# Block 1 of an attention and PReLU kernel: tile steps spaced out, loads between norm products, q of batch 0 first

## The chip, the cores and the metric

The kernel runs on one core of a Trainium2 chip. The metric is device time in microseconds of one execution; 301.3 us is the median of the five runs of the kernel before.

## The reference

Inputs q, k, v have shape (8, 8, 576, 64): batch, heads, sequence, head dimension. The result has 4608 rows of 512.

```python
kv = einsum('bhsd,bhse->bhde', k, v)
out = einsum('bhsd,bhde->bhse', q, kv)
rms = sqrt(mean(out * out, axis=-1, keepdims=True) + 1e-06)
x = (out / rms * g_norm).transpose(0, 2, 1, 3).reshape(4608, 512)
h = x @ w_in                                   # 512 -> 2048
g = maximum(h, 0) + alpha * minimum(h, 0)
result = g @ w_out                             # 2048 -> 512
```

## The kernel before

Each engine's instructions are in an order written out by hand. PE is TensorE, DVE VectorE, ACT ScalarE, POOL GpSimd; SP issues the transposes and stores, POOL the loads.

**Blocks.** The 4608 rows of x are cut into nine blocks w = 0 to 8 of 512 rows. A batch has 576 rows, so a block holds parts of two batches. A block's first layer is 16 groups g (`m1_group`): four matmuls of 128x512 into a PSUM buffer h_ps (three of them, in turn), then ACT writes m_sb = relu(-h) (L474), and DVE writes gt = m_sb * beta + h (L476). The second layer of the block before (`y_mm`, L494) is put between the groups of the block, four matmuls after each group. Block 1 is different: the second layer of block 0 was mostly done ahead of it, so between its 16 groups there is little else for PE.

**Attention.** For batches 0 and 1 (`NB_PE = 2`) it is done at the start, with transposed outputs: `step_t` transposes q on PE, `step_kv` makes k^T v of head pairs (L240) and masks it on DVE into kv_sb (L244), `step_ot` multiplies by q, `ssq_mm` and `norm` normalize. For the later batches it is done a block ahead, in tiles of 128 rows, in steps laid between the groups (`phase_steps`):

- `tile_a`: four matmuls into otm_ps on PE (L387), and the square on ACT.
- `tile_b`: the sums of squares by a DVE reduce (L399).
- `tile_c`: Ln and Exp on ACT, then rg = rstd * g on POOL (L411, the norm product).
- `tile_d`: xrow = otm_ps * rg on DVE (L420), and a DMA transpose of xrow on SP's queue into xm, the input of the next block (L425).

In one step, tile_b and tile_d come ahead of the group's own instructions, tile_c and step_kv behind its matmuls, tile_a at the end. Before the change, a tile's a, b with c, and d are in three steps in a row. Block 1 has the tiles of batch 2 that block 2 needs: three, with tile_a after groups 7, 8 and 9. kv of batch 2 is made behind group 5.

**Loads.** q, k, v are loaded with a cast to 16 bits by POOL's queue, two issues for each tensor of a batch (`load`: 64 partitions of five rows, 64 partitions of four). There are two stage buffers, so batch b + 2 takes the place of batch b. `regroup` copies q and k so that a pair of heads lies together (on DVE up to batch 2, on POOL after it, L106); `transpose_q` then transposes q by DMA into qtm. In block 1, POOL waits at `gate` (L677) for the transposed q of batch 2, then issues q and k of batch 3; its v follows behind group 9. Batch 4 is loaded in block 2 by six issues in a row ahead of group 6.

**Start.** Batch 0 is loaded in halves of four heads, in the order q, k, v, q, k, v. `keep_warm` issues matmuls whose result nobody uses. `spread_g` makes g_all, which tile_c reads, by one matmul (g_ps, L522) behind group 12 of block 0.

Of the kernel before, what the change touches and what calls it, by code (L numbers as in the profile page):

```python
# [9 lines left out]
FP32 = mybir.dt.float32  # L10
# [7 lines left out]
def kernel(  # L18
# [11 lines left out]
    nc = tc.nc  # L30

    B, H, S, D = q.shape
# [3 lines left out]
    P = 128  # L36
# [4 lines left out]
    TPP = S // P  # L41
    REM = S - TPP * P
    NT = TPP + 1
# [46 lines left out]
    def zero_rest(st):  # L90
        nc.vector.memset(st[REM:P, :, TPP, :], 0.0)

    def load(b, nm, h0=0, h1=H):
        st = stages[b % NBUF][nm][:, h0:h1]
        src = srcs[nm][b, h0:h1]
        nc.gpsimd.dma_start(
            out=st[0:REM].rearrange("p h t d -> p h (t d)"),
            in_=src[:, 0:LONG, :].rearrange("h (p t) d -> p h (t d)", t=NT),
        )
        nc.gpsimd.dma_start(  # L100
            out=st[REM:P, :, 0:TPP, :].rearrange("p h t d -> p h (t d)"),
            in_=src[:, LONG:S, :].rearrange("h (p t) d -> p h (t d)", t=TPP),
        )

    def regroup(b, nm, h0=0, h1=H, eng=None):
        (eng or nc.vector).tensor_copy(  # L106
            out=bufs[b % NBUF][nm][:, :, h0:h1, :].rearrange("p t h d -> p h t d"),
            in_=stages[b % NBUF][nm][:, h0:h1],
        )
# [6 lines left out]
        for nm in ("q", "k"):  # L116
            regroup(b, nm, eng=nc.gpsimd)

    for nm in "qkv":
        zero_rest(stages[0][nm])  # L120
    HH = H // 2
    load(0, "q", 0, HH)

    ident = const_p.tile([P, P], FP32, name="ident")
    make_identity(nc, ident[:])
    for h0 in (0, HH):
        for nm in "qkv":
            if (h0, nm) != (0, "q"):
                load(0, nm, h0, h0 + HH)

    mask32 = const_p.tile([P, P], FP32, name="mask32")
    nc.vector.memset(mask32[:], 0.0)
# [11 lines left out]
    nc.vector.tensor_copy(out=ident16[:], in_=ident[:])  # L144
    for nm in "kvq":
        zero_rest(stages[1][nm])

    g2col = const_p.tile([P, 1], FP32, name="g2col")
    nc.sync.dma_start(out=g2col[0:64, :], in_=g_norm[:].unsqueeze(1))
# [47 lines left out]
    def keep_warm(n):  # L197
        for i in range(n):
            nc.tensor.matmul(  # L199
                out=warm_ps[:], lhsT=mask16[:], rhs=warm16[:], start=True, stop=True,  # L200
            )
# [10 lines left out]
    def step_t(b, j, pool=(ps_s, "s"), eng=None):  # L212
        qs = pair_cols(b, "q", j)
        qt_ps = pool[0].tile([P, NT * P], FP16, name="qt_ps", tag=pool[1])
        for t in range(NT):
            nc.tensor.matmul(
                out=qt_ps[:, t * P : (t + 1) * P],
                lhsT=qs(t),
                rhs=ident16[:],
                is_transpose=True,  # L220
                start=(t == 0),
                stop=(t == NT - 1),
            )
        qts[b, j] = attn_p.tile([P, S], FP16, name="qt_sb", tag=f"qt{j}")
        if eng is nc.scalar:
            nc.scalar.copy(out=qts[b, j][:], in_=qt_ps[:, 0:S])
        else:
            nc.vector.tensor_copy(out=qts[b, j][:], in_=qt_ps[:, 0:S])
# [26 lines left out]

    def square(sq, ot_ps, shape, eng):
        if eng is nc.vector:
            o_sb = attn_p.tile(shape, FP32, name="o_sb", tag="rg")
            nc.vector.tensor_copy(out=o_sb[:], in_=ot_ps[:])
            nc.vector.tensor_mul(out=sq[:], in0=ot_ps[:], in1=o_sb[:])  # L260
        else:
            nc.scalar.activation(out=sq[:], in_=ot_ps[:], func=AF.Square)
# [141 lines left out]
    def tile_c(b, t):  # L404
        n, _, ss = tiles[b, t]
        nc.scalar.activation(  # L406
            out=ss[0:n], in_=ss[0:n], func=AF.Ln, bias=eps_t[0:n], scale=inv_d,
        )
        nc.scalar.activation(out=ss[0:n], in_=ss[0:n], func=AF.Exp, bias=0.0, scale=-0.5)  # L409
        rg = attn_p.tile([P, H, D], FP32, name="rg")  # L410
        nc.gpsimd.tensor_tensor(  # L411
            out=rg[0:n], in0=ss[0:n].unsqueeze(2).to_broadcast([n, H, D]),
            in1=g_all[0:n].unsqueeze(1).to_broadcast([n, H, D]), op=ALU.mult,
        )
        tiles[b, t][2] = rg
# [14 lines left out]
    def phase_steps(w):  # L430


        if w >= NW:
            return []
        todo = [(b, t) for b in range(NB_PE, min(B, w + 1)) for t in range(NT)
                if (b, t) not in done and b * S + t * P < (w + 1) * W]
        done.update(todo)
        steps = []

        kv_at = {NB_PE: 5, NB_PE + 1: 3}.get(w, 0)  # L440
        if w == NB_PE:
            n = NPAIR // JT
            for i in range(n + 1):
                m = [lambda i=i: step_tail_ot(i)] if i < n else []
                m += [lambda i=i: step_tail_ssq(i - 1)] if i > 0 else []
                steps.append(([], [], m))
        n = {NB_PE: 7, NB_PE + 1: 2}.get(w, 0)
        steps += [([], [], []) for i in range(n - len(steps))]
        for i in range(len(todo) + 2):
            a, b, d = ([todo[i - k]] if 0 <= i - k < len(todo) else [] for k in range(3))  # L450
            begin = [lambda x=x: tile_b(*x) for x in b] + [lambda x=x: tile_d(*x) for x in d]
            mid = [lambda x=x: tile_c(*x) for x in b]
            end = [lambda x=x: tile_a(*x) for x in a]
            steps.append((begin, mid, end))
        if w < B:
            steps[kv_at][1].append(lambda: step_kv(w))
        return steps
# [60 lines left out]

    def spread_g():

        g_ps = ps_y.tile([P, D], FP32, name="g_ps", tag="y")
        nc.tensor.matmul(  # L522
            out=g_ps[:], lhsT=ones32[0:D], rhs=diag[0:D], start=True, stop=True,
        )
        nc.vector.tensor_copy(out=g_all[:], in_=g_ps[:])
# [7 lines left out]
    )  # L533
    step_t(0, 0, H_POOL[0])
    step_t(0, 1, H_POOL[1], nc.scalar)
    regroup(0, "k", 0, HH)
    keep_warm(8)
    step_kv(0, 0, 2)
# [1 line left out]
    step_ot(0, 0)  # L540
    step_ot(0, 1)
    keep_warm(1)
    regroup(0, "q", HH, H)
    ssq_mm(0, 0)
    step_t(0, 2, H_POOL[2])
    step_t(0, 3, H_POOL[0])
# [8 lines left out]
        out=beta_sb[:], in0=alpha_ps[:], scalar1=-1.0, scalar2=1.0, op0=ALU.mult, op1=ALU.add,  # L555
    )
    ssq_mm(0, 1)
    regroup(0, "k", HH, H)
    norm(0, 0)
    keep_warm(3)  # L560
    step_kv(0, 2, 4)
    keep_warm(2)
    load_batch(2)
# [22 lines left out]
              13: (ps_s, "s")}  # L586
    for g in range(5, NF):
        m1_group(0, g, others.get(g))
        if g == 12:
            spread_g()  # L590

# [42 lines left out]
    ssq_mm(1, 3, S_POOL)  # L634
    norm(1, 2)
    ahead(11, NF)
    norm(1, 3)
    regroup(2, "q")
    transpose_q(2)
    for a in range(TPW - 1):  # L640
        y_out(ys[a], 0, a, nc.vector if a == 1 else None)

# [5 lines left out]
    for w in range(1, NW):  # L648
        steps = phase_steps(w + 1)
        for g in range(NF):  # L650
            if g == LOAD_G and 3 < w + 2 < B:
                load_batch(w + 2)
            a, part = divmod(g, TPW)
            parts = range(part * TPW, (part + 1) * TPW)
            if w == 1:
                a, y = TPW - 1, ys[TPW - 1]
                parts = [LATER + g] if LATER + g < NF else []
            begin, mid, end = steps.pop(0) if steps else ([], [], [])
            for f in begin:
                f()  # L660
            m1_group(w, g)
            for f in mid:
                f()
            if 0 in parts:
                pool, tag = ((ps_y, "y"), (ps_s, "s"))[a % 2]
                y = pool.tile([P, W], FP32, name="y_ps", tag=tag)
            for gg in parts:
                y_mm(y, w - 1, a, gg)
            if NF - 1 in parts:
                y_out(y, w - 1, a)  # L670
            for f in end:
                f()
            if (w, g) == (1, 3):


                gate = const_p.tile([1, 1], FP16, name="gate")
                nc.gpsimd.tensor_copy(out=gate[:], in_=qtms[2][0:1, 0, 0:1])  # L677
                load(3, "q")
                load(3, "k")
                regroup(2, "k")  # L680
            if (w, g) == (1, 9):
                load(3, "v")
            if g == (13 if w == 1 else LOAD_G + 3) and w + 2 < B:
                regroup_batch(w + 2)
            if g == (15 if w == 1 else NF - 3) and w + 2 < B:
                transpose_q(w + 2)
# [43 lines left out]
```

## Time and profile before

| | us |
|---|---|
| Runs shown | 301.42, 300.75, 300.70, 301.44, 301.30 |
| Median | 301.3 |
| Profiled execution | 301.42 |
| Its span, first to last instruction | 299.3 |
| PE busy | 284.0 (95%) |
| DVE busy | 169.6 (57%) |
| ACT busy | 152.7 (51%) |
| POOL busy | 97.8 (33%) |

The span lies inside the profiled execution; the 2.1 us around it hold no instruction. Busy shares are averages over stages: the start is bound by loads, from block 2 on PE is full. A stage's own rows say what bounds it.

### The profile page before, as it was taken

To read this page: it belongs to the slowest core of one execution; us is meant where nothing else is said; L and a number is where in the kernel's file an instruction comes from. 1 tells how busy PE (TensorE), PEld (TensorE's weight loads), DVE (VectorE), ACT (ScalarE), POOL (GpSimd) and SP (SyncE) were. 2 spreads that over 40 slices of the span, in tenths; PEclk is the share of its full clock that TensorE was granted. 3 is DMA by queue.
4 is the path that set the end of the run, shared out by engine and by line. 5 is a ranking of instruction groups with operands and counts; after the bars stand their busy time and mean duration, and the time that the engine had idled before them with its cause. 6 is when DMAs were issued, how large, how long until landed. Compare 5 with 4: busy or idle time off the path is not lost.

```text
span 299.3 us, 4290 instructions
## 1 busy us (share of the span) xinstructions
PE 284.0 (95%) x1552; PEld 138.4 (46%) x1552; DVE 169.6 (57%) x262; ACT 152.7 (51%) x297; POOL 97.8 (33%) x109
## 2 busy tenths in 40 slices
PE   5889999987999999999999999999999999999994
PEld 2444454542453454445544544454445444444443
DVE  5468846785485458445954584468546744344200
ACT  1458355773475457435843573368347644443311
POOL 8843410349059415541466164515002300000000
PEclk9999999995999999999999999999999999999998
DMA  6999999999329943993399449926211411112232
GB/s 81 167 206 204 199 206 198 192 194 170 68 63 150 229 103 81 154 227 70 81 133 227 107 79 142 248 59 90 61 35 37 96 35 37 35 37 51 54 71 70
DMA packets 66228, 35.54 MB, mean 119 GB/s; under 512 B 32784, under 2 KB 61728, under 8 KB 66208
## 3 DMA queue, kind: packets, MB, share of 16 engines
q0 software_dynamic: 29664, 18.35, 44.5%
q1 hardware_dynamic: 36384, 16.80, 27.5%
q8 instruction: 12, 0.20, 0.3%
q10 hardware_dynamic: 160, 0.13, 0.2%
q14 instruction: 8, 0.07, 0.1%
HBM read 36.71 MB, written 9.44 MB: 154 GB/s over the span
## 4 chain that ended last, share of the span: by engine, by line
PE 76%; DMA 11%; POOL 4%; DVE 4%; issue 2%; ACT 1%; DVEq 0%; POOLq 0%; ACTq 0%
PE y_ps L494 35%; PE h_ps L467 32%; DMA qst<-in_q_dram 5%; DMA w_in_sb<-in_moe_w_in_dram 3%; PE kv_ps L240 3%; DMA vst<-in_v_dram 2%; POOL rg L411 2%; PE otm_ps L387 2%; DMA xm<-xrow 2%; DVE gt L476 1%; PE yb L494 1%; PE ya L494 1%; PE yc L494 1%; PE yd L494 1%; DVE ksb L106 1%
## 5 line engine op out<-in xcount | busy, mean ns | idle before, releaser
L476 DVE SCALAR_TENSOR_TENSOR gt<-m_sb,beta_sb,h_ps 128x512 f16<-128x512 f32 x144 | 105.6, 744 | 78.7 <-ACT m_sb L474 78.0
L474 ACT ACTIVATE m_sb<-h_ps 128x512 f32<-128x512 f32 x144 | 85.5, 597 | 91.2 <-PE h_ps L467 90.4
L494 PE MATMUL y_ps<-w_out_sb,gt 128*128 128x512 f16 (+1 forms) x528 | 128.8, 373 | 0.0
L467 PE MATMUL h_ps<-xm,w_in_sb 128*128 128x512 f16 x448 | 115.0, 379 | 1.4 <-DVE gt L476 0.7
L494 PEld LDWEIGHTS <-gt 128*128 128x128 f16 x592 | 57.6, 98 | 64.7
L467 PEld LDWEIGHTS <-w_in_sb 128*128 128x128 f16 x584 | 56.1, 99 | 67.1 <-issue 9.1
L411 POOL TENSOR_TENSOR rg<-ss,g_all 128x512 f32<-128x512 f32 (+1 forms) x30 | 31.3, 1047 | 87.1 <-ACT ss L409 83.7
L467 PE MATMUL h_ps<-xt,w_in_sb 128*128 128x512 f16 (+1 forms) x136 | 32.6, 387 | 2.8 <-DVE gt L476 2.8
L504 ACT COPY y_sb<-y_ps 128x512 f32<-128x512 f32 (+1 forms) x32 | 18.4, 575 | 16.3 <-PE y_ps L494 16.3
L399 DVE TENSOR_REDUCE ss<-sqm_sb 128x8 f32<-128x512 f32 (+1 forms) x30 | 20.5, 682 | 9.3 <-ACT sqm_sb L393 9.2
L420 DVE TENSOR_TENSOR xrow<-otm_ps,rg 128x512 f16<-128x512 f32 (+1 forms) x30 | 20.4, 682 | 7.1 <-POOL rg L411 7.1
L393 ACT ACTIVATE sqm_sb<-otm_ps 128x512 f32<-128x512 f32 (+1 forms) x30 | 17.7, 591 | 7.4 <-PE otm_ps L387 7.4
L106 POOL COPY qsb<-qst 128x2560 f16<-128x2560 f16 x5 | 11.6, 2320 | 11.6 <-issue 10.9
L106 POOL COPY ksb<-kst 128x2560 f16<-128x2560 f16 x5 | 11.6, 2321 | 4.9 <-DMA kst<-in_k_dram 4.9
L387 PEld LDWEIGHTS <-qtm 128*128 128x128 f16 x120 | 9.2, 98 | 7.1
L240 PE MATMUL kv_ps<-vst,ksb 128*128 128x128 f16 x160 | 10.4, 219 | 2.1 <-DMA vst<-in_v_dram 1.7
L240 PEld LDWEIGHTS <-ksb 128*128 128x128 f16 x160 | 9.5, 98 | 4.9 <-issue 1.4
L387 PE MATMUL otm_ps<-kv_sb,qtm 128*128 128x128 f16 x120 | 11.6, 219 | 0.0
L199 PE MATMUL warm_ps<-warm,mask 128*128 128x512 f16 x26 | 8.5, 468 | 3.3 <-DVE eps_t L142 3.3
L406 ACT ACTIVATE ss<-ss,eps_t 128x8 f32<-128x8 f32 (+1 forms) x30 | 9.0, 301 | 3.2 <-DVE ss L399 3.1
L244 DVE TENSOR_TENSOR kv_sb<-kv_ps,mask 128x512 f16<-128x512 f32 (+1 forms) x9 | 5.6, 628 | 4.8 <-PE kv_ps L240 4.7
L502 DVE COPY y_sb<-y_ps 128x256 f32<-128x256 f32 x1 | 0.4, 424 | 13.4 <-PE y_ps L494 13.4
(75 smaller groups left out, 136.9 us busy)
## 6 DMA issues: line engine op xcount, KB each, us to landing
out_dram<-y_sb SPq DMA_DIRECT2D x70, 128.0 KB, 2.4
kst<-in_k_dram POOLq DMA_DIRECT2D x7, 320.0 KB, 8.8
qst<-in_q_dram POOLq DMA_DIRECT2D x7, 320.0 KB, 5.0
vst<-in_v_dram POOLq DMA_DIRECT2D x7, 320.0 KB, 10.6
w_in_sb<-in_moe_w_in_dram POOLq DMA_DIRECT2D x4, 512.0 KB, 10.5
w_out_sb<-in_moe_w_out_dram POOLq DMA_DIRECT2D x4, 512.0 KB, 15.4
kst<-in_k_dram POOLq DMA_DIRECT2D x7, 256.0 KB, 9.5
qst<-in_q_dram POOLq DMA_DIRECT2D x7, 256.0 KB, 6.9
```

The costliest lines, as they stand in the source:

```text
L106: (eng or nc.vector).tensor_copy(out=bufs[b % NBUF][nm][:, :, h0:h1, :].rearrange("p t h d -> p h t d"), in_=stages[b % NBUF][nm][:, h0:h1],)
L240: nc.tensor.matmul(out=kv_ps[:, j - j0, :], lhsT=ks(t), rhs=vs(t), start=(t == 0), stop=(t == NT - 1),)
L387: nc.tensor.matmul(out=ot_ps[:, 2 * j : 2 * j + 2, :], lhsT=qtms[b][:, t * NPAIR + j, :], rhs=kvs[b, j], start=True, stop=True,)
L393: nc.scalar.activation(out=sq[0:n], in_=ot_ps[0:n], func=AF.Square)
L399: nc.vector.tensor_reduce(out=ss[0:n], in_=sq[0:n], op=ALU.add, axis=mybir.AxisListType.X,)
L411: nc.gpsimd.tensor_tensor(out=rg[0:n], in0=ss[0:n].unsqueeze(2).to_broadcast([n, H, D]), in1=g_all[0:n].unsqueeze(1).to_broadcast([n, H, D ...
L420: nc.vector.tensor_mul(out=x[0:n], in0=ot_ps[0:n], in1=rg[0:n])
L467: nc.tensor.matmul(out=h_ps[:, cols], lhsT=w_in_blk(c, g), rhs=xt_of(w, c)[:, cols], start=(c == 0), stop=(c == NC - 1 and cols.stop == W),)
L474: nc.scalar.activation(out=m_sb[:], in_=h_ps[:], func=AF.Relu, scale=-1.0)
L476: nc.vector.scalar_tensor_tensor(out=gt[:], in0=m_sb[:], scalar=beta_sb[:, g : g + 1], in1=h_ps[:], op0=ALU.mult, op1=ALU.add,)
L494: nc.tensor.matmul(out=y[:], lhsT=gts[w, g][:, a * P : (a + 1) * P], rhs=w_out_blk(g)[:, cols], start=(g == 0), stop=(g == NF - 1),)
L504: nc.scalar.copy(out=y_sb[:, cols], in_=y[:])
```

## The change

- Batch 0: q is loaded whole, in two issues, ahead of k and v in halves. The identity is made behind the first half of k. The memset of q's rest moves behind those of batch 1's buffers. The second half of q is regrouped right behind the first transposes.
- `spread_g` moves into the start, in place of one `keep_warm` matmul, with another PSUM buffer.
- The regroup and transpose of q of batch 2 go ahead of the last `norm` of block 1's input; the regroup of k of batch 2 moves from behind group 3 to behind group 1.
- Block 1: kv behind group 4, tile_a behind groups 5, 6, 7, tile_b and tile_c two groups later, tile_d three after that. rg has three buffers. v of batch 3 is issued behind group 10, its regroups behind group 12.
- Block 2: the six loads of batch 4 are issued one by one behind groups 4 to 9; its regroups follow behind group 10.

On POOL, the v loads of batch 3 now come behind the third rg (before: behind the second). In block 2 the order is rg, rg, load, rg, load, rg, load, rg, three loads (before: rg three times, six loads, rg twice).

```diff
-    for nm in "qkv":
-        zero_rest(stages[0][nm])
     HH = H // 2
-    load(0, "q", 0, HH)
+    load(0, "q")
+    for nm in "kv":
+        zero_rest(stages[0][nm])
+    load(0, "k", 0, HH)
     ident = const_p.tile([P, P], FP32, name="ident")
     make_identity(nc, ident[:])
-    for h0 in (0, HH):
-        for nm in "qkv":
-            if (h0, nm) != (0, "q"):
-                load(0, nm, h0, h0 + HH)
+    load(0, "v", 0, HH)
+    load(0, "k", HH, H)
+    load(0, "v", HH, H)
...
     for nm in "kvq":
         zero_rest(stages[1][nm])
+    zero_rest(stages[0]["q"])
...
-        rg = attn_p.tile([P, H, D], FP32, name="rg")
+        rg = attn_p.tile([P, H, D], FP32, name="rg", bufs=3)
...
-        kv_at = {NB_PE: 5, NB_PE + 1: 3}.get(w, 0)
+        kv_at = {NB_PE: 4, NB_PE + 1: 3}.get(w, 0)
...
-        n = {NB_PE: 7, NB_PE + 1: 2}.get(w, 0)
+        n = {NB_PE: 5, NB_PE + 1: 2}.get(w, 0)
         steps += [([], [], []) for i in range(n - len(steps))]
-        for i in range(len(todo) + 2):
-            a, b, d = ([todo[i - k]] if 0 <= i - k < len(todo) else [] for k in range(3))
+        lags = (0, 2, 5) if w == NB_PE else (0, 1, 2)
+        for i in range(len(todo) + lags[2]):
+            a, b, d = ([todo[i - k]] if 0 <= i - k < len(todo) else [] for k in lags)
...
-        g_ps = ps_y.tile([P, D], FP32, name="g_ps", tag="y")
+        g_ps = ps_s.tile([P, D], FP32, name="g_ps", tag="s")
...
     step_t(0, 1, H_POOL[1], nc.scalar)
+    regroup(0, "q", HH, H)
     regroup(0, "k", 0, HH)
...
     keep_warm(1)
-    regroup(0, "q", HH, H)
     ssq_mm(0, 0)
...
     ssq_mm(0, 1)
+    spread_g()
     regroup(0, "k", HH, H)
     norm(0, 0)
-    keep_warm(3)
+    keep_warm(2)
...
         m1_group(0, g, others.get(g))
-        if g == 12:
-            spread_g()
...
-    norm(1, 3)
     regroup(2, "q")
     transpose_q(2)
+    norm(1, 3)
...
-            if g == LOAD_G and 3 < w + 2 < B:
+            if g == LOAD_G and 4 < w + 2 < B:
                 load_batch(w + 2)
...
                 load(3, "q")
                 load(3, "k")
+            if (w, g) == (1, 1):
                 regroup(2, "k")
-            if (w, g) == (1, 9):
+            if (w, g) == (1, 10):
                 load(3, "v")
-            if g == (13 if w == 1 else LOAD_G + 3) and w + 2 < B:
+            if w == 2 and 4 <= g < 10:
+                load_part(4, "qkv"[(g - 4) // 2], g % 2 == 0)
+            if g == (12 if w == 1 else LOAD_G + 3 + (w == 2)) and w + 2 < B:
                 regroup_batch(w + 2)
```

`load_part` is one of the two issues of `load`.

More of the change, by code (lines that the diff above doesn't have):

```diff
@@ L91, in zero_rest, with load_part, load @@
         nc.vector.memset(st[REM:P, :, TPP, :], 0.0)
-    def load(b, nm, h0=0, h1=H):
+    def load_part(b, nm, long, h0=0, h1=H):
         st = stages[b % NBUF][nm][:, h0:h1]
         src = srcs[nm][b, h0:h1]
[L96 to L103, printed above, removed]
+        if long:
+            nc.gpsimd.dma_start(
+                out=st[0:REM].rearrange("p h t d -> p h (t d)"),
+                in_=src[:, 0:LONG, :].rearrange("h (p t) d -> p h (t d)", t=NT),
+            )
+        else:
+            nc.gpsimd.dma_start(
+                out=st[REM:P, :, 0:TPP, :].rearrange("p h t d -> p h (t d)"),
+                in_=src[:, LONG:S, :].rearrange("h (p t) d -> p h (t d)", t=TPP),
+            )
+    def load(b, nm, h0=0, h1=H):
+        load_part(b, nm, True, h0, h1)
+        load_part(b, nm, False, h0, h1)
     def regroup(b, nm, h0=0, h1=H, eng=None):
@@ L117, in regroup_batch @@
             regroup(b, nm, eng=nc.gpsimd)
-    for nm in "qkv":
+    HH = H // 2
+    load(0, "q")
+    for nm in "kv":
         zero_rest(stages[0][nm])
-    HH = H // 2
-    load(0, "q", 0, HH)
+    load(0, "k", 0, HH)
     ident = const_p.tile([P, P], FP32, name="ident")
     make_identity(nc, ident[:])
-    for h0 in (0, HH):
-        for nm in "qkv":
-            if (h0, nm) != (0, "q"):
-                load(0, nm, h0, h0 + HH)
+    load(0, "v", 0, HH)
+    load(0, "k", HH, H)
+    load(0, "v", HH, H)
     mask32 = const_p.tile([P, P], FP32, name="mask32")
@@ L257, in square @@
         if eng is nc.vector:
-            o_sb = attn_p.tile(shape, FP32, name="o_sb", tag="rg")
+            o_sb = attn_p.tile(shape, FP32, name="o_sb", tag="rg", bufs=3)
             nc.vector.tensor_copy(out=o_sb[:], in_=ot_ps[:])
```

## The prediction

> **What bounds the kernel now.** First the page's slices: PE is near full but for the start and one place.
>
> ```profile
> PE   5889999987999999999999999999999999999994
> ...
> PEclk9999999995999999999999999999999999999998
> ```
>
> Each digit covers 7.5 us. PE loses in the ninth and tenth, 60 to 75 us, and in the tenth the granted clock is halved. I then asked for the busy time by stage (columns: stretch, length, then busy us of each engine, clock, DMA share, GB/s).
>
> ```profile
> 65.00:67.00 2.00, 0.98 (x6) 0.34 (x5) 2.00 (x4) 1.48 (x4) 1.16 (x2) 1.00 1.36 213
> 67.00:69.00 2.00, 1.17 (x5) 0.42 (x4) 1.34 (x3) 1.48 (x4) 1.89 (x3) 0.90 1.67 163
> 69.00:71.00 2.00, 1.10 (x3) 0.30 (x2) 1.37 (x3) 0.60 (x1) 2.00 (x2) 0.50 1.03 137
> ```
>
> From 65 us PE is half idle, while DVE, POOL and DMA are in use. The timeline of that place, by engine (start and length in us; in brackets the idle time before and who ended it), says who waits.
>
> ```profile
> 64.07 1.04 POOL L411 TENSOR_TENSOR rg<-ss,g_all 128x512 f32<-128x512 f32 x1 [3.43 <-DVE gt L476]
> 65.84 1.04 POOL L411 TENSOR_TENSOR rg<-ss,g_all 128x512 f32<-128x512 f32 x1 [0.73 <-ACT ss L409]
> 67.11 0.74 POOL L96 DMA_DIRECT2D vst<-in_v_dram  x1 [0.22 <-issue]
> 67.83 0.70 POOL L100 DMA_DIRECT2D vst<-in_v_dram  x1
> 68.52 1.07 POOL L411 TENSOR_TENSOR rg<-ss,g_all 128x512 f32<-128x512 f32 x1
> ...
> 66.55 1.02 PE L467 MATMUL h_ps<-xt,w_in_sb 128*128 128x512 f16 x4 [1.02 <-DVE gt L476]
> 68.40 1.70 PE L467 MATMUL h_ps<-xt,w_in_sb 128*128 128x512 f16 x4 [0.83 <-DVE gt L476]
> 71.03 3.57 PE L467 MATMUL h_ps<-xt,w_in_sb 128*128 128x512 f16 x8 [0.93 <-DVE gt L476]
> 75.22 1.11 PE L467 MATMUL h_ps<-xm,w_in_sb 128*128 128x512 f16 x4 [0.62 <-DMA xm<-xrow]
> ...
> 69.63 0.69 DVE L420 TENSOR_TENSOR xrow<-otm_ps,rg 128x512 f16<-128x512 f32 x1 [1.28 <-POOL rg L411]
> ```
>
> The third norm product rg (L411) stands behind two load issues (1.44 us) on POOL. Its xrow stands at the head of DVE's queue and waits 1.28 us; the gt behind it hold back PE. But the end of the stage is set elsewhere: block 2 (75.22) waits for xm, the DMA transpose of that last xrow. The DMA issues of that stretch, one transpose each, end with the us from issue to landing:
>
> ```profile
> xm<-xrow SPq DMA_TRANSPOSE x1, 4.2
> ...
> xm<-xrow SPq DMA_TRANSPOSE x1, 6.8
> ...
> xm<-xrow SPq DMA_TRANSPOSE x1, 4.7
> ```
>
> The last, issued at 70.35, landed at 75.05. So this stage is worth what the last transpose gains, not PE's lost time. The timeline of block 2 shows a second, smaller case:
>
> ```profile
> 94.30 0.69 DVE L420 TENSOR_TENSOR xrow<-otm_ps,rg 128x512 f16<-128x512 f32 x1 [3.17 <-POOL rg L411]
> 95.70 1.02 PE L467 MATMUL h_ps<-xm,w_in_sb 128*128 128x512 f16 x4 [0.74 <-DVE gt L476]
> ```
>
> Six load issues (89.07 to 93.2) stand ahead of an rg. DVE loses 3.17 us, PE only 0.74.
>
> [...] clock 0.90 and 0.50 above put the fall at 68.6, and 0.90 in 75 to 77 the return at 75.4[...]. It now falls where PE waits anyway. [...] between 60 and 100 us the landings of xm were 2.4 to 7.2 us, the short ones without loads beside them.
>
> **The change part by part.**
>
> 1. *Start: q of batch 0 whole and first.* The first k-v product (10.70) now waits for four half tensors instead of three. Halves landed at 6.1, 8.5, 10.6 and 12.5 us (issue in the timeline and landing time in the DMA view), so it is up to 1.9 us late. Against this, DMA moved only 84 GB/s in 2.5 to 4.5 and 137 in 4.5 to 6.5, against 183 at 12.5; larger first transfers and ident moved behind k may bring the stream about 1 us forward: product at 11.6 to 12.6. From there the chain in order is: product 0.55, semaphore 0.2, kv_sb 0.42, ot 0.2, two squares 1.1, ssq 0.2, Ln and Exp 1.3, norm 0.74, the second kv_sb 0.42 (behind that norm on DVE), half_ot, its square and ssq 1.3, with about 0.2 at each change of engine 7.2 in all: the first w_in matmul comes at 18.8 to 19.8 instead of 18.5. Before, v of the second half (15.8) and w_in (18.2) covered part of this. Cost 0.3 to 1.3, taken 0.8. The memset of q's rest costs nothing: 0.27 us on DVE, done by 5 us, ahead of the landing of q. Two fewer load issues (0.6 each) on POOL are hidden too: the loads after them wait for landings.
>
> 2. *spread_g moved, one keep_warm less.* The g_ps matmuls open a gap of 0.45 us in a full PE row at 30.2; in the start they take the place of a warm matmul (0.22). Gain 0.45. Parts 1 and 2 leave +0.35 for the start of block 1, as PE is full from there on.
>
> 3. *regroup(2, q) and its transpose ahead of norm(1, 3).* q of batch 2 lands at 48.8; the regroup now starts there and not at 50.09, and its 6.3 us transpose lands at 56 instead of 57.2. The POOL gate behind it and the loads of q and k of batch 3 start 1.2 earlier (issue at 57.75, last landing 69.4 before, about 68 now). On SP nothing stands ahead of the transpose; the y stores behind it are not waited for. norm(1, 3) slips from 49.42 to 49.65; the matmul on it starts at 51.9: hidden.
>
> 4. *Block 1.* The k regroup is two groups earlier, kv at group 4, tiles at groups 5 to 7, reduces at 7 to 9, xrow at 10 to 12, both v loads behind all three rg. No xrow waits for POOL then, but DVE holds the same work. I lay it out from the xm norm (55.53), with the steps between DVE starts of this trace (0.60 to 0.66 a piece, regroup 0.73): regroup 56.2, gt2 to gt4 to 58.9, kv_sb 58.9, gt5 59.9, then 1 us idle, since PE's first tile waits about 0.6 us for kv_sb with only one group between (two before): gt6 61.6, reduce 62.2, gt7, reduce 63.5, gt8 64.5, reduce, gt9, xrow 66.4, gt10, xrow 67.6, gt11, third xrow 68.9. Against 69.63 that is 0.7 earlier; with the 0.35 of the start, 69.3. So the last transpose is issued at 70.0, not 70.35: the waits on rg go, but one gt more stands before the last xrow, and the idle DVE after kv_sb is new. PE is done with its groups at about 71.5 instead of 74.6. Each transpose holds SP for 1.2, less than the 1.25 between xrows, so SP adds nothing. The regroups of q and k of batch 3 and the q transpose follow the v loads on POOL as before, about 0.5 earlier; first needed after 80. The landing decides. An estimate: it takes 2.4 without loads and 4.7 as before; q and k are through earlier, v (issued at about 68) is beside it. I take the middle, 3.6: landing 73.6. Against 75.22, gain 1.6; from both ends 0.0 (4.7 and a start 0.5 worse) to 2.8.
>
> 5. *Block 2: loads of batch 4 one by one.* Between two rg on POOL now stands one issue of 0.72. Period of a step 1.95, rg 1.04 and issue 0.72 are 1.76: it fits. The 0.74 of PE is gained; POOL's regroups come as before (at about 96), and the q transpose behind them has until block 3. Bounds 0.4 to 0.8.
>
> 6. The three rg buffers cost no time; there are more tiles in flight, in PSUM too (three of three tags), and the next tile comes only in block 2.
>
> Sum: block 2 starts 1.6 earlier (the start's 0.35 is counted in that), and 0.74 goes inside it; after it PE has no idle time, so both reach the end: 1.6 + 0.7 = 2.3 us. The profiled execution takes 301.42 with a span of 299.3; 301.4 - 2.3 = 299.1. The median shown, 301.3, is 0.1 lower, well inside the runs' 0.74.
>
> **Rivals.**
>
> *A: as summed*, 299.1 (own range 298.0 to 300.3). For it: each wait named is in the trace.
>
> *B: the clock falls later.* PE now stops at 71.5 and waits 2.1 us for xm. [...] Before, the halved time was hidden under the DVE stall. Against it: in 10.5 to 16.5 us PE is busy 1.2 to 1.7 of each 2 us and keeps the clock. Then 300.8.
>
> *C: slower, the clock again, with a transpose that gains nothing*. The v loads are issued at 68, just when the transposes come; the second one before took 6.8 us in that place. With a start 1.3 late and 4.7 or more to land, block 2 starts at 75.2 or later, PE waits over 3 us[...]: 302.5. [...]
>
> *D: better*: start late by 0.3 alone and a landing in 2.4: block 2 at 72.0, PE hardly idle: 301.4 - 3.2 - 0.74 = 297.5.
>
> **How the numbers follow.** A 0.47, B 0.2, C 0.2, D 0.13. A measurement here tells 0.2%, 0.6 us, from no change. Faster (under 300.7): nearly all of A, D, a third of B: 0.65. Same: over half of B, some of A and C: 0.14. Slower: most of C, a bit of B: 0.21. The range 297.6 to 302.3 leaves out the outer halves of D and C. Likeliest: A.
>
> **What would show it.** In the new profile: no xrow with a wait on rg over 0.3 us in blocks 1 and 2; the third xrow near 69.3; block 2's first matmul at 73 to 74, waiting for xm; the first w_in matmul at about 19.3; no g_ps gap. Wrong, if block 2 starts after 75, if PEclk shows a 5 in the slices after 75 us, or if the start loses over 1.3.

## The result and the profile after

The changed kernel is slower by a little: 302.75 us median of 43 runs (301.57 to 304.14) against 301.45 for the kernel before, a ratio of 1.0042 [1.003, 1.0054]. The forecast was 299.1. The profiled execution took 304.03 us with a span of 301.9, 2.6 more than the span before; it is one of the longer runs. The runs lie around two centres, 24 with a median of 302.4 and 19 with one of 303.8, without a clear gap between them; the part on the start below has a candidate for what parts them.

The same two rows of slices, 7.5 us each, of the changed kernel (busy tenths of PE, granted clock):

```profile
PE   4889999984899999999999999999999999999994
PEclk9799999998699999999999999999999999999999
```

PE's tenth slice, 67.5 to 75 us, has fallen from 7 to 4, and the eleventh from 9 to 8. In the kernel before, the clock fell in the tenth slice (and a little in the last); now it is low in the second and from the tenth into the eleventh, where PE has full work. The stretch by stages of 2 us (length, busy us of PE, of PE's weight loads, of DVE, ACT, POOL, then clock, DMA share, GB/s):

```profile
65.00:67.00 2.00, 1.50 (x8) 0.59 (x7) 1.67 (x4) 1.47 (x5) 1.58 (x2) 1.00 1.10 154
67.00:69.00 2.00, 1.54 (x8) 0.54 (x6) 2.00 (x4) 1.75 (x5) 1.42 (x2) 1.00 0.00 0
69.00:71.00 2.00, 1.77 (x8) 0.61 (x7) 2.00 (x4) 0.73 (x2) 2.00 (x3) 1.00 0.59 76
71.00:73.00 2.00, 1.03 (x5) 0.29 (x3) 1.57 (x4) 1.20 (x2) 2.00 (x2) 1.00 1.25 159
73.00:75.00 2.00, 0.00 (x0) 0.00 (x0) 0.67 (x1) 0.00 (x0) 1.61 (x1) 0.73 1.35 160
75.00:77.00 2.00, 0.09 (x1) 0.12 (x2) 0.00 (x0) 0.00 (x0) 0.00 (x0) 0.50 1.32 218
77.00:79.00 2.00, 2.00 (x6) 0.61 (x6) 0.00 (x0) 0.19 (x1) 0.00 (x0) 0.50 0.92 206
79.00:81.00 2.00, 2.00 (x7) 0.76 (x6) 0.75 (x1) 0.40 (x1) 0.00 (x0) 0.56 0.00 0
```

Read down PE: 1.50 to 1.77 where it had 0.98 to 1.17, so the DVE stalls are gone, and then next to nothing for over 4 us. Read down the DMA share: 0.00 from 67 to 69, while POOL has norm products to do, then a long stretch at work until almost 79. The clock, last but two: 0.73 in 73 to 75 puts its fall at 73.9, and 0.56 in 79 to 81 its return at 80.7. The timeline of POOL and DVE, and of PE at the start of block 2 (start and length in us; in brackets the idle time before and its releaser):

```profile
67.41 1.04 POOL L418 TENSOR_TENSOR rg<-ss,g_all 128x512 f32<-128x512 f32 x1 [0.48 <-ACT ss L416]
68.63 0.73 POOL L97 DMA_DIRECT2D vst<-in_v_dram  x1 [0.17 <-PE h_ps L476]
69.35 0.68 POOL L102 DMA_DIRECT2D vst<-in_v_dram  x1
69.84 0.68 DVE L427 TENSOR_TENSOR xrow<-otm_ps,rg 128x512 f16<-128x512 f32 x1
...
76.91 1.86 PE L476 MATMUL h_ps<-xm,w_in_sb 128*128 128x512 f16 x4 [4.65 <-DMA xm<-xrow]
78.57 1.91 PE L503 MATMUL y_ps<-w_out_sb,gt 128*128 128x512 f16 x4
80.27 1.26 PE L476 MATMUL h_ps<-xm,w_in_sb 128*128 128x512 f16 x4
82.24 1.03 PE L476 MATMUL h_ps<-xm,w_in_sb 128*128 128x512 f16 x4
```

No xrow of this block waits for rg any more. But v of batch 3 is issued at 68.63, where it was issued at 67.11 before, and block 2 starts at 76.91 instead of 75.22. Its first matmuls then take 1.86 us for four, and 1.03 from 82.24 on: half clock on full work. The view of the tile xm in this stretch gives the landing of the three transposes:

```profile
DMA to landing us min/median/max: 3.9/6.1/7.0
```

The first (issued at 68.0, ahead of v) took 3.9, the second 7.0, the last 6.1: issued at 70.7, landed at 76.8. An estimate of the 2.6 us between the two traces: block 1 starts 0.87 later (52.16 against 51.29); block 2 starts 1.69 later in all, those 0.87 among them; half clock on full work from 76.9 to 80.7, 3.8 us at half speed, 1.9; less what block 2 gains, 0.74 (the wait of PE that is gone there). That makes 2.85, 0.25 more than the spans differ by.

### The profile page after: what moved, and what is told of

The parts are those of the page before. It is cut to its first block, busy times and chain, and to the rows that moved or that the text cites. A ratio compares the mean times of both kernels' runs of the same rounds, so it can differ in the third digit from the quotient of the medians.

```text
span 301.9 us, 4284 instructions
## 1 busy us (share of the span) xinstructions
PE 284.5 (94%) x1551; PEld 138.5 (46%) x1551; DVE 169.2 (56%) x262; ACT 152.7 (51%) x297; POOL 97.0 (32%) x107
## 4 chain that ended last, share of the span: by engine, by line
PE 86%; DVE 5%; DMA 4%; ACT 2%; issue 1%; POOL 0%; DVEq 0%; POOLq 0%
PE h_ps L476 38%; PE y_ps L503 37%; PE kv_ps L247 3%; PE otm_ps L394 2%; DMA xm<-xrow 2%; DMA qst<-in_q_dram 2%; DVE gt L485 2%; PE warm_ps L206 1%; PE ya L503 1%; PE yb L503 1%; PE yc L503 1%; DVE ksb L112 1%; DVE kv_sb L251 1%; PE qt_ps L223 1%; PE yd L503 1%
## 5 line engine op out<-in xcount | busy, mean ns | idle before, releaser
L476 PE MATMUL h_ps<-xt,w_in_sb 128*128 128x512 f16 (+1 forms) x136 | 30.3, 366 | 1.4 <-DVE gt L485 1.4
L513 ACT COPY y_sb<-y_ps 128x512 f32<-128x512 f32 (+1 forms) x32 | 18.4, 575 | 16.3 <-PE y_ps L503 16.0
L112 POOL COPY qsb<-qst 128x2560 f16<-128x2560 f16 x5 | 11.6, 2320 | 11.0 <-issue 9.6
L112 POOL COPY ksb<-kst 128x2560 f16<-128x2560 f16 x5 | 11.6, 2321 | 8.3 <-DMA kst<-in_k_dram 8.3
L206 PE MATMUL warm_ps<-warm,mask 128*128 128x512 f16 x25 | 9.3, 520 | 3.0 <-DVE eps_t L148 3.0
L394 PE MATMUL otm_ps<-kv_sb,qtm 128*128 128x128 f16 x120 | 11.6, 219 | 0.4 <-DVE kv_sb L251 0.4
```

The lines of the kernel that those rows point to most:

```text
L112: (eng or nc.vector).tensor_copy(out=bufs[b % NBUF][nm][:, :, h0:h1, :].rearrange("p t h d -> p h t d"), in_=stages[b % NBUF][nm][:, h0:h1],)
L394: nc.tensor.matmul(out=ot_ps[:, 2 * j : 2 * j + 2, :], lhsT=qtms[b][:, t * NPAIR + j, :], rhs=kvs[b, j], start=True, stop=True,)
L476: nc.tensor.matmul(out=h_ps[:, cols], lhsT=w_in_blk(c, g), rhs=xt_of(w, c)[:, cols], start=(c == 0), stop=(c == NC - 1 and cols.stop == W),)
L513: nc.scalar.copy(out=y_sb[:, cols], in_=y[:])
```

## The experiments

In each the median is set against that of the kernel before on the same chip, with the 95% interval of the ratio. My theory after the result: what decides is when the loads of batch 3 are through, since the transposes were slow to land beside them (4.2 to 6.8 us in the kernel before, 3.9 to 7.0 in the changed one; the transpose issued at 86.2 in the kernel before, with no load packet under way, took 2.4); the change had moved the last of these loads, v, behind the third rg. The rivals were the idle time of PE and its clock alone, the later start, and the tile steps themselves.

### The issue of v: moved in both kernels

**The move alone, in the kernel before:**

```diff
-            if (w, g) == (1, 9):
+            if (w, g) == (1, 10):
                 load(3, "v")
```

> The kernel before, with one edit: v of batch 3 is issued behind group 10 of block 1, that is behind the third rg and not behind the second, as the change does. Theory (the last xm transpose is served when the last load of batch 3 is through; in all traces so far block 2 starts 1.0 to 2.3 us after that): v is issued at about 68.3 and not 67.1, its last packet ends near 74.6, block 2 starts at 76 and PE waits longer: 301.2 + 1.0 = 302.2 us, although no xrow waits for POOL any more. Rival (the wait of xrow on rg is the cost): the third xrow is 1.3 us earlier and so is block 2: 300.3 us.

Measured: 303.58 against 301.34, 1.006 [1.0034, 1.0087]: this one line makes the kernel before 2.2 us slower by the medians, 1.8 by the ratio. From its timeline:

```profile
68.27 0.69 DVE L420 TENSOR_TENSOR xrow<-otm_ps,rg 128x512 f16<-128x512 f32 x1 [0.47 <-POOL rg L411]
68.46 0.74 POOL L96 DMA_DIRECT2D vst<-in_v_dram  x1 [0.22 <-issue]
69.18 0.70 POOL L100 DMA_DIRECT2D vst<-in_v_dram  x1
75.72 1.87 PE L467 MATMUL h_ps<-xm,w_in_sb 128*128 128x512 f16 x4 [4.17 <-DMA xm<-xrow]
```

The third xrow is 1.36 earlier than in the kernel before (69.63; 0.8 of this is an earlier first w_in matmul in this profile, 17.69 against 18.49), its wait on rg is 0.47 instead of 1.28, and still block 2 starts 0.5 later, at half clock. Taking away the wait that the prediction saw on POOL made it worse, because v is now loaded later.

**The move undone, in the changed kernel** (v between the second and the third rg again):

```diff
-            if (w, g) == (1, 10):
+            if (w, g) == (1, 8):
                 load(3, "v")
```

> The changed kernel, with v of batch 3 issued behind group 8, between the second and the third rg, as in the kernel before. Theory: v is issued at about 66.9 and not 68.6, the last load ends 1.6 us earlier, block 2 starts at 75.3 and not 76.9; the third rg ends at 69.9, about when its xrow is due, and costs little: 302.75 - 1.6 = 301.1 us. Rival: the third rg delays its xrow and the transpose, nothing is gained: 302.7 us.

Measured: 300.59 against 301.34, 0.9965 [0.9943, 0.9986]; 2.2 us less than the changed kernel. With v back in its place the rest of the change is a gain of 0.7. Its timeline shows that the wait for the transpose has only become shorter:

```profile
65.47 0.74 POOL L97 DMA_DIRECT2D vst<-in_v_dram  x1 [0.17 <-issue]
68.22 0.69 DVE L427 TENSOR_TENSOR xrow<-otm_ps,rg 128x512 f16<-128x512 f32 x1
74.00 1.26 PE L476 MATMUL h_ps<-xm,w_in_sb 128*128 128x512 f16 x4 [3.37 <-DMA xm<-xrow]
```

The third xrow is at 68.22; its transpose is issued at 69.2 and takes 4.7. Here too the profile has an earlier first w_in matmul than the changed kernel's (18.3 against 20.0).

**v right behind q and k of batch 3, in the changed kernel:**

```diff
                 load(3, "q")
                 load(3, "k")
+                load(3, "v")
...
-            if (w, g) == (1, 10):
-                load(3, "v")
```

> The changed kernel, with v of batch 3 issued right behind q and k of batch 3 (behind group 3 of block 1) and not behind the third rg. Theory: the v loads, issued at 68.6 us, are what keeps the last two xm transposes from landing (6 us after issue). Then v is through by about 69 us, the last transpose (issued at 70.9) lands in 2.4 to 3 us, block 2 starts at 73.5 and not at 76.9, PE waits about 1.3 us and not 4.65, the clock does not fall: 302.75 - 3.4 - 1.9 = 297.5 us. Rival: the transposes land 5 to 6 us after issue whatever else moves: block 2 at 76 to 77, 302 to 303 us.

Measured: 297.71 against 301.24, 0.9883 [0.9846, 0.992]: 5.0 us less than the changed kernel, 3.5 less than before. The stages of this run:

```profile
67.00:69.00 2.00, 1.54 (x8) 0.50 (x7) 2.00 (x4) 1.75 (x5) 1.53 (x2) 1.00 1.38 193
69.00:71.00 2.00, 1.77 (x8) 0.67 (x7) 2.00 (x4) 0.78 (x2) 2.00 (x2) 1.00 1.04 156
71.00:73.00 2.00, 1.08 (x5) 0.29 (x3) 1.57 (x4) 1.20 (x2) 2.00 (x1) 1.00 0.48 95
73.00:75.00 2.00, 1.73 (x9) 0.82 (x10) 0.77 (x2) 0.60 (x1) 0.03 (x1) 1.00 0.96 186
```

and the landing of its three transposes:

```profile
DMA to landing us min/median/max: 2.4/2.4/3.2
```

PE's work from 67 to 71 us is the same to the hundredth (1.54, 1.77), as is DVE's. The third xrow is even 0.06 later, at 69.90. What differs is DMA: in use from 67 to 69 where it had 0.00, and through with the loads at 70.2. The last transpose then takes 2.4 instead of 6.1, block 2 starts at 73.27, and the clock stays at 1.00. How the loads and the transposes mix is seen in the DMA view from 68 to 77 us, 40 slices of 0.22 us (busy tenths, then GB/s), first of the changed kernel, then of the one with v early:

```profile
DMA  0000039935646799999999999999999999999999
GB/s 0 0 0 0 0 72 222 213 76 17 23 14 26 83 103 177 151 148 191 191 178 175 153 145 146 170 173 114 170 180 180 179 184 207 175 130 272 291 238 288
```

```profile
DMA  9999999998329960049920059999999999999100
GB/s 200 190 193 200 198 170 222 221 178 111 42 57 209 210 122 0 0 99 224 213 47 0 0 124 223 212 205 217 221 212 221 215 221 213 221 215 178 17 0 0
```

With v early the loads fade out by 70.3, and each later transpose is a burst of about 0.6 us above 200 GB/s with nothing beside it. In the changed kernel there is one such burst too, from 69.1 to 69.9, with v just issued; then for 0.9 us only 14 to 26 GB/s move, and the second and third transposes land after 76.

The view of the DMA queues tells the loads (q0) from the transposes (q1): packets, MB, share of the 16 engines, in the changed kernel from 69.9 to 72.5 us, and then from 73.5 to 75:

```profile
q0 software_dynamic: 394, 0.25, 89.5%
q1 hardware_dynamic: 45, 0.00, 2.3%
...
q0 software_dynamic: 330, 0.17, 88.5%
q1 hardware_dynamic: 306, 0.08, 51.7%
```

The second transpose was issued at 69.3 and the third at 70.7, yet up to 72.5 their queue moves next to no bytes; from 73.5 on the two queues move nearly as many packets each. The 0.9 us of low rate are something else: the beginning of v's own loads. In the same trace the loads of later batches begin slowly too, with no packet of another queue beside them (stages of 1 us, the last two at the beginning of such loads):

```profile
70.00:71.00 1.00, 1.00 (x4) 0.37 (x4) 1.00 (x2) 0.39 (x1) 1.00 (x2) 1.00 0.55 21
122.60:123.60 1.00, 1.00 (x6) 0.42 (x5) 0.75 (x1) 0.07 (x1) 1.00 (x2) 1.00 0.91 46
182.10:183.10 1.00, 1.00 (x6) 0.41 (x5) 0.75 (x1) 0.07 (x1) 1.00 (x2) 1.00 0.75 26
```

So v issued by itself begins slowly a second time, and v right behind q and k does not: there the loads ran on at 193 GB/s from 67 to 69. How much of the 5.0 us comes from this and how much from the transposes that no longer wait was not separated by any run.

**v early in the kernel before** (the same edit, with the issue taken from behind group 9):

> The kernel before, with one edit: v of batch 3 issued right behind q and k of batch 3 and not behind group 9. Theory (the v loads set the landing of the last xm transpose): the third rg no longer stands behind two issues and v is through by about 70 us, so the third xrow comes at about 68.3 and its transpose lands in about 2.5 us: block 2 starts at 72 and not at 75.2, 301.3 - 3 = 298.3 us. Rival (the wide spacing of the tile steps is needed for the gain): DVE still waits on rg, the clock falls at 68.6 as before and PE is the last to come: 300.5 us or more.

Measured: 301.7 against 301.09, 1.0004 [0.9981, 1.0027], runs from 299.95 to 303.73: nothing gained, where 298.3 was expected. So the early issue alone isn't enough, against my theory in its first form. In its trace (300.29, one of its shorter runs) v is issued at 59.9, but the first transposes are issued while loads still run, and the loads are through only at 72.4; block 2 starts at 74.28 after PE has waited 2.87.

**One table over the traces** shows what goes with the start of block 2. "Loads through" is the end of the last packet of batch 3's loads in the trace.

| kernel | issue of v | third xrow | loads through | block 2 |
|---|---|---|---|---|
| before | 67.11 | 69.63 | 73.40 | 75.22 |
| changed | 68.63 | 69.84 | 75.70 | 76.91 |
| before, v behind the third rg | 68.46 | 68.27 | 74.78 | 75.72 |
| changed, v between rg 2 and 3 | 65.47 | 68.22 | 72.26 | 74.00 |
| before, v with q and k | 59.91 | 68.13 | 72.39 | 74.28 |
| changed, v with q and k | 58.94 | 69.90 | 70.23 | 73.27 |

In the rows where the loads end after the third xrow by 2 us or more, block 2 follows the last load packet by 0.9 to 1.9 us, whatever the xrow did (in the eight traces that the table leaves out, by 1.0 to 2.3). Only in the last row do the transposes set the time themselves: third xrow to block 2 is 3.4 there, and 5.6 to 7.5 in the others. The edits moved the issue of v; that the transposes wait for the end of the loads is my reading of these times, and no run isolated it.

### The block 1 part alone

The kernel before with the new order around norm(1, 3), kv_at, lags, rg buffers and the issues of block 1, and nothing of the start, spread_g or block 2:

```diff
-        kv_at = {NB_PE: 5, NB_PE + 1: 3}.get(w, 0)
+        kv_at = {NB_PE: 4, NB_PE + 1: 3}.get(w, 0)
...
+        lags = (0, 2, 5) if w == NB_PE else (0, 1, 2)
...
-            if (w, g) == (1, 9):
+            if (w, g) == (1, 10):
                 load(3, "v")
```

> The kernel before, with only the block 1 part of the change: wide tile steps, kv at group 4, three rg buffers, the regroups and v of batch 3 at their new places, q of batch 2 transposed ahead of the last norm. Theory: the last transpose lands no earlier, PE waits some 4 us for it at full stop, and the clock falls in block 2: 301.3 + 1.5 = 302.8 us. Rival: the start makes the changed kernel slower, block 1 alone is no worse: 301.3 or less.

Measured: 304.22 against 301.09, 1.0087 [1.0053, 1.0121]. The loss of the whole change is in this part and is larger here, 2.6 us by the ratio and 3.1 by the medians. From the view of PE's waits (in all, times, longest):

```profile
PE h_ps L475 <- DMA xm<-xrow: 4.6, 1, 4.6
```

It is the wait of the changed kernel to a tenth, with the old start. So the new start is not what makes it.

### The idle PE and the clock

16 unused matmuls between the last group of block 1 and the first of block 2, in the changed kernel:

```diff
         steps = phase_steps(w + 1)
+        if w == 2:
+            w2_ps = ps_y.tile([P, W], FP32, name="w2_ps", tag="y")
+            for i in range(16):
+                nc.tensor.matmul(out=w2_ps[:], lhsT=mask16[:], rhs=warm16[:], start=True, stop=True)
```

> The changed kernel, with 16 matmuls whose result nobody uses (3.5 us) between the last group of block 1 and the first of block 2, where PE waits 4.65 us for xm. Theory: the half clock from 76.9 to 80.7 us costs 1.9 us; PE stays busy enough, the clock stays whole, block 2 starts at 76.9 as before: 302.75 - 1.9 = 300.9 us. Rival: the half clock costs nothing, since later waits take it up: 302.7 us. If the clock still falls: 302.7 us and PEclk shows it.

Measured: 301.0 against 301.24, 0.9997 [0.997, 1.0025], 1.75 less than the changed kernel. Its slices and the start of block 2:

```profile
PEclk9999999999999999999999999999999999999999
...
74.97 1.02 PE L476 MATMUL h_ps<-xm,w_in_sb 128*128 128x512 f16 x4 [0.92 <-DMA xm<-xrow]
```

Keeping PE at work through the wait gives back about what was put down to the clock, 1.9. The wait itself is about as it was: issue of v to block 2 takes 8.0 us (66.97 to 74.97), 8.3 in the changed kernel. (Both ends are earlier than there, as the first w_in matmul came at 18.41 in this profile and at 20.0 in the other.) So the loss has two terms that go together, the later transposes and the clock (0.50 on full work after 4.65 us of idle PE, no fall with the 16 matmuls and 0.92 of waiting), and the clock is not the first cause: with v early the same PE work needs no such matmuls.

### The start, spread_g and block 2 by themselves

**The start alone**, in the kernel before:

```diff
-    load(0, "q", 0, HH)
+    load(0, "q")
...
-    for h0 in (0, HH):
-        for nm in "qkv":
-            if (h0, nm) != (0, "q"):
-                load(0, nm, h0, h0 + HH)
+    load(0, "v", 0, HH)
+    load(0, "k", HH, H)
+    load(0, "v", HH, H)
```

> The kernel before, with only the start of the change: q of batch 0 whole and first, its second half regrouped early, the memset moved; spread_g stays behind group 12. Theory: the first w_in matmul starts 1.5 us later (20.0 and not 18.5, as in the changed kernel), and as PE and the DVE chain of block 1 follow it, everything up to block 2 is later by 1.3: 302.7 us. Rival: loads of batches 1 and 2 set block 1, the start is covered: 301.4 us.

Measured: 301.07 against 301.24, 0.9988 [0.9959, 1.0016]; no cost that can be told from none, where 1.3 us were expected. Its first w_in matmul came at 17.89. In the changed kernel's profile it came at 20.0, and the timeline of PE there shows where the time went:

```profile
8.54 0.81 PE L223 MATMUL qt_ps<-ident,qsb 128*128 128x128 f16 x10 [1.94 <-DVE qsb L112]
9.14 3.54 PE L206 MATMUL warm_ps<-warm,mask 128*128 128x512 f16 x8
```

PE waits 1.94 us for the whole q, the clock is at half from 9.1 to 12.5, and eight unused matmuls take 3.54 us. In the trace with the start alone the same wait was 1.45:

```profile
8.60 0.73 PE L217 MATMUL qt_ps<-ident,qsb 128*128 128x128 f16 x10 [1.45 <-DVE qsb L106]
9.17 1.89 PE L200 MATMUL warm_ps<-warm,mask 128*128 128x512 f16 x8
```

There the same eight take 1.89, 1.65 less. The length of the wait alone doesn't decide it: in the profile with v early it was 1.16, and still the eight took 3.04 and the first w_in matmul came at 19.95. I take the clock at the start for what parts the changed kernel's runs, whose two centres lie 1.4 apart; only one of its runs was traced, so this is argued, not shown.

**spread_g alone** (another PSUM buffer, moved to behind ssq_mm(0, 1), one keep_warm less):

```diff
-    keep_warm(3)
+    spread_g()
+    keep_warm(2)
...
-        if g == 12:
-            spread_g()
```

> The kernel before, with only spread_g moved into the start in place of one unused matmul. Theory: the gap of 0.45 us in block 0 goes, and PE, DVE and the v issue of block 1 (which stands behind an rg) are all earlier by it: 300.8 us. Rival: loads set the end of block 1 whatever PE does: 301.2 us.

Measured: 301.22 against 301.34, 1.0012 [0.9991, 1.0034]; the interval leaves the expected gain of 0.45 out. Its trace is of one of its longer runs (302.79). In it block 1 does start 0.6 earlier (50.69 against 51.29), but block 2 starts at 75.26, as before, and the clock, halved since 68.0, stays low into block 2:

```profile
75.00:77.00 2.00, 1.74 (x5) 0.66 (x6) 0.40 (x1) 0.00 (x0) 0.00 (x0) 0.50 1.13 255
77.00:79.00 2.00, 2.00 (x8) 0.77 (x7) 0.75 (x1) 0.60 (x1) 0.00 (x0) 0.69 0.00 0
```

In this execution the gain ahead of a wait that didn't move made the wait longer (PE's wait for xm is 1.27 instead of 0.62). That the shorter runs lose the gain in the same way is not shown.

**The loads of batch 4 one by one**, in the kernel before:

```diff
-            if g == LOAD_G and 3 < w + 2 < B:
+            if g == LOAD_G and 4 < w + 2 < B:
                 load_batch(w + 2)
...
+            if w == 2 and 4 <= g < 10:
+                load_part(4, "qkv"[(g - 4) // 2], g % 2 == 0)
```

> The kernel before, with only the six loads of batch 4 spread over groups 4 to 9 of block 2 and its regroups behind group 10. Theory: the DVE wait of 3.17 us on rg and the PE wait of 0.74 us at 95 us go: 301.45 - 0.7 = 300.7 us. Rival: each rg is a little late and PE loses the same: 301.4 us.

Measured: 300.63 against 301.24, 0.9975 [0.9945, 1.0004]: 0.6 less, with an interval that just reaches no change. (The regroups of batch 4 moved with it, as in the change.) The changed kernel's own trace shows the step in the timeline of block 2:

```profile
93.44 1.04 POOL L418 TENSOR_TENSOR rg<-ss,g_all 128x512 f32<-128x512 f32 x1
94.43 0.72 POOL L97 DMA_DIRECT2D kst<-in_k_dram  x1
94.54 0.68 DVE L427 TENSOR_TENSOR xrow<-otm_ps,rg 128x512 f16<-128x512 f32 x1
94.83 1.03 PE L476 MATMUL h_ps<-xm,w_in_sb 128*128 128x512 f16 x4
```

The xrow comes without an idle DVE before it, and the matmul without an idle PE.

### What the early v needs

**Early v with the old start** (the changed kernel, spread_g moved, loads of batch 0 as before):

```diff
-    load(0, "q")
+    load(0, "q", 0, HH)
...
+                load(3, "v")
```

> The changed kernel with v of batch 3 early and the start of the kernel before (q, k, v in halves; spread_g stays in the start). Theory: the old start has no long gap on PE, so no run has its first w_in matmul at 20 us: 297.0 us with a narrow spread. Rival: the new start is the better one when the clock holds, and the old one is 0.5 us longer: 297.7 to 298.2 us.

Measured: 301.47 against 301.09, 0.9991 [0.9962, 1.002], runs from 298.44 to 302.71. The gain of 3.5 is gone, where 297.0 was expected. In its trace, which is of one of its longest runs (302.52), the gate for batch 3's loads comes at 56.7 instead of 55.5, the loads are through at 72.35 instead of 70.23, and block 2 starts at 74.60 at half clock. A delay of 1.2 us at their beginning becomes 2.1 at their end, and the transposes (third xrow at 68.59) now fall among them: issued from 66.8 to 69.4, they took 5.1 to 6.2 to land, against 2.4 to 3.2 for those issued from 68.1 to 70.7 with the new start.

**Four more unused matmuls at the start**, with v early:

```diff
-    keep_warm(10)
+    keep_warm(14)
```

> The changed kernel with v of batch 3 early, and 14 in place of 10 unused matmuls at the very start. Theory: in the changed start PE is idle from 6.6 to 8.5 us, [...] (first w_in matmul at 20.0 and not at 18.4): about 4 in 10 runs are 1.5 us longer. With the gap filled all runs are of the short kind: 297.0 us and a narrower spread. Rival: the first k-v product waits for v, not for the clock, and the start stays as it is: 297.7 us.

Measured: 297.77 against 301.09, 0.9889 [0.985, 0.9927], six runs. In its profile PE's wait for q is 0.46 and the clock holds at the start (first w_in matmul at 18.41), but the median is that of the version without it (297.71). Inconclusive with so few runs.

**tile_d one group earlier as well**, on top of the early v and the 14 matmuls:

```diff
-        lags = (0, 2, 5) if w == NB_PE else (0, 1, 2)
+        lags = (0, 2, 4) if w == NB_PE else (0, 1, 2)
```

> The changed kernel with v of batch 3 behind its q and k, 14 unused matmuls at the start, and tile_d two groups behind tile_b instead of three. Theory: with v out of the way the last xrow sets block 2; one gt less stands before it, 0.6 us or more, the third rg ends just in time: 297.7 - 0.7 = 297.0 us. Rival: the xrows wait for rg again and DVE holds back PE: 297.7 us or more.

Measured: 297.71 against 301.34, 0.9879 [0.9858, 0.99], runs from 297.08 to 298.3. In its trace the third xrow is at 67.71, 2.2 earlier than with v early alone in that version's trace (69.90; 1.4 of this is an earlier first w_in matmul, 18.59 against 19.95). Block 2 comes at 72.02, 1.25 earlier and so less than the xrow: the last transpose, now issued at 68.5 with loads running to 69.95, takes 3.4 instead of 2.4. Against the version with 14 matmuls, which differs in nothing else, the third xrow is 0.64 earlier and block 2 0.39. The three versions with v early, the wide tile steps and the new start are the best of the study, 1.1 to 1.2% faster than the kernel before, and can't be told apart.

## Why the prediction was wrong

**The step that failed** is in part 4, "An estimate: it takes 2.4 without loads and 4.7 as before; ... I take the middle, 3.6: landing 73.6". The last transpose took 6.1. Inside block 1 everything ahead of this term held. With block 1 starting 0.87 late instead of 0.35, the schedule gives the third xrow at 69.8 and the end of PE's groups at 72.0; measured 69.84 and 72.26. So xrow, DVE, PE and POOL were right, and the price of the DMA behind them was wrong by 2.5 us. The longer wait brought a second cost that the sum put at nothing, the half clock on full work, 1.9. With the 0.5 by which the start was worse, this makes 4.9, which is what lies between 299.1 and the profiled 304.03.

The bounds were wrong too. I let the landing lie between two values that had been seen, though the trace of the kernel before showed 6.8 for the transpose issued closest to v, and I moved v 1.5 us later, towards the last one. The text noted that v "is beside it" and still took a middle. What the runs show in its place: block 2 follows the end of the loads (by 0.9 to 1.9 us in five of the table's six traces), and the place of v's issue moves that end (70.23 to 75.70 in the changed kernel). The move of v from behind the second rg to behind the third, listed under part 4 as a detail, was the change's largest term, +2.2 us in the kernel before and -2.2 when undone.

Behind that lies an assumption of mine that no trace had shown: that a transpose has a share of the DMA beside the loads from its issue on. In the changed kernel's trace the two queues do move nearly equal numbers of packets from 73.5 to 75 us (330 and 306), but from 69.9 to 72.5 the waiting transposes moved next to nothing (45 packets, where the loads moved 394). Together this is 3.9 to 7.0 to land, where the last transpose of the trace with v early, issued when the loads were through, took 2.4.

**Rival C was the case that came**, 302.5 against 302.75: "the v loads are issued at 68, just when the transposes come", and "the clock again". What it said came in: block 2 at 76.9, a wait of PE of over 3 us, and a low clock on full work. It was also off in part: it had the transpose gain nothing, where it took 6.1 instead of 4.7. What its sum took for the clock was an estimate of mine that no trace had shown; read from the changed kernel's trace, the half clock took 1.9. Since block 2 came 1.7 later than C had it and the total still fits, the closeness of the two totals is partly luck: the profiled run, with all these terms in it, took 304.03. I gave it 0.2 because the case "as summed" named only waits that the trace showed. But a wait that is removed says nothing of what takes its place on another queue.

**The clock.** It was low from 73.9 to 80.7 us in the changed kernel, 6.8 us, and from 9.1 to 12.5, 3.4 us, at its start; in the kernel before from 68.6 to 75.4, also 6.8. What sets when it falls and for how long was not shown by these runs. Rivals B and C had it fall again, on my estimate alone. B was right that the low time would be later and no longer hidden: from 77 to 79 PE was busy for all 2.00 us at a clock of 0.50.

**The start.** Taken 0.8, bounds 0.3 to 1.3. The first w_in matmul came at 20.0 in the changed kernel's profile, 1.5 late and outside, with the half clock in it; the working did not look at PE's own wait for the whole q (1.94). With the clock held the matmul came at 17.9 (start alone) to 18.4 (with the unused matmuls) and cost nothing. The chain priced at 7.2 us took 7.0 to 7.5; it was the product ahead of it that was mis-sized: 10.94 with the clock held, where 11.6 to 12.6 was forecast. The 12.52 of the changed kernel's profile lies in the forecast range by luck, as the forecast had no clock in it.

**spread_g.** "Gain 0.45" was about right for its place (block 1 0.6 earlier in the one trace) and wrong for the end; in that trace the wait behind it took it. The same holds for part 3: the gate came at 55.46, 1.8 earlier than before and more than the 1.2 predicted, but v did not use it. The 0.00 of DMA from 67 to 69 shows this head start unused.

**Block 2.** "The 0.74 of PE is gained": measured 0.6 by itself, with an interval that just reaches no change, and no wait of PE there in the changed kernel's trace. This fits.

## What to carry to other kernels

When a stage ends with a DMA transpose that runs beside loads, don't price the transpose as if it ran alone (2.4 us here, and 3.9 to 7.0 beside loads in the changed kernel). In these traces the end of the loads told more: list every load issued before the transpose is through and ask when the last of them lands. Moving a DMA issue out of the way of a compute instruction moved its whole transfer too (v issued 1.5 us later in the changed kernel, its last packet 2.3 later), so look for a place ahead of the stall, right behind other loads where there are some (POOL had 5.6 us idle ahead of its first norm product, and DMA 2 us of nothing) before one behind it. And a gain on an engine that then waits is not only void: the longer idle time can cost the clock when the work comes back (in the changed kernel 4.65 us of idle PE, then 3.8 us of full work at 0.50).

## What the runs showed of the hardware that was not expected

A transpose of 128 KB landed in 2.4 us by itself (the last one with v early) and in 3.9 to 7.0 in the changed kernel, with loads beside it. In the longest of these it stood still first: from 69.9 to 72.5 the transposes' queue moved 45 packets and next to no bytes, while the loads moved 394. Where the last loads ran beside transposes, they ended later: with v early and the old start, they began 1.2 us later and ended 2.1 later. That transposes stood still behind loads was seen in the traces, and its cause was not isolated; the one pair of runs that moved the transposes with the issues of the loads left alone (tile_d one group earlier or not, 14 matmuls in both) moved them by 0.64 us only, for which the last took 3.4 instead of 3.1. So it stays open.

Loads that began after a stretch without loads began slowly: 21, 46 and 26 GB/s in the microsecond at 70.0, 122.6 and 182.1 us of the changed kernel's trace, against 193 from 67 to 69 with v early, in the middle of a row of loads. DMA was 0.55 to 0.91 busy in those microseconds, so there the rate said more than the busy share. What the slow beginning comes from is open too.

A low clock in the first 10 us did not follow the length of PE's wait alone: after 1.94 us the eight matmuls took 3.54 and after 1.16 they took 3.04, but after 1.75 and 1.45, in two other kernels, 1.89. What decides it was not shown.
